# Two linear-attention blocks under one gate: the upper half of block A's q by seven products, woven with k chunks and a block of x^T phi(k)

## The chip, the cores and the metric

The kernel runs on one core of one Trainium2 chip. The metric is the device time of one execution in microseconds (us). Three runs of the kernel before took 188.43, 188.61 and 189.28, a median of 188.61.

## The reference

Two attention blocks, A and B, get the same x (2048 rows, 640 columns, bfloat16) with weights of their own. A gate mixes their outputs row by row:

```python
x = A_x
g = _sigmoid((x * gate_w).sum(-1, keepdims=True))
...
    phi = lambda t: jnp.where(t > 0, t + 1, jnp.exp(t)) + 1e-6
    pq, pk = phi(q), phi(k)
    kv = jnp.einsum("bhsd,bhse->bhde", pk, v)
    z = jnp.einsum("bhsd->bhd", pk)
    num = jnp.einsum("bhqd,bhde->bhqe", pq, kv)
    den = jnp.einsum("bhqd,bhd->bhq", pq, z)[..., None] + 1e-6
    o = num / den
...
return g * a + (1 - g) * b
```

q, k and v are x times a third of wqkv each, in 32 heads of 20 columns; a and b are o times wo of the block.

## The kernel before

**What is computed in which form.** v is never formed: kv is wv^T times G, where G = x^T phi(k) is 640 by 640. phi(k) lies in `pk` as 16 chunks of 128 rows, phi(q) transposed in `pqT[b]` as five blocks m of 128 features by 2048 rows. x lies in `xn` by rows and in `xT` transposed, in five blocks c of 128 columns. The gate's logits come from an extra column of A's k weights (column 320 of the second half) and are carried as `gl`, then `gf`.

**k.** `k_chunk` makes one of the 16 chunks: ten matmuls of 320 columns (L284) into a pair of PSUM banks (a slot), then phi. ScalarE (ACT) takes exp into `e` (L258), VectorE (DVE) clamps it (L263, "clamp"), and DVE takes the maximum of q + 1 and e (L272, "top"), reading PSUM. In the "lifted" form ACT also writes q + 1 to SBUF (L260), and DVE's top is a maximum of two bfloat16 tensors in SBUF (L267). The slot is then free once ACT has read it.

**q.** `q_unit` makes one block m for 1024 rows: ten matmuls of 512 columns (L336) and phi. `q_strassen` makes two blocks, m and m + 2, for the same 1024 rows by seven products in place of eight (Strassen's method, in the form with four sums on each side), for the contraction blocks c 0 to 3; block c = 4 is added in the ordinary way. That is 18 matmuls (L392) instead of 20. Its left sums are differences of weights, `TQ` (`tq_sums`, L376), its right ones sums of x^T, `SQ` (`sq_sum`, L369). It uses four single banks, `quad` = ce, cf, co, cz. A first product in ce is copied to co by ACT (L416); cz gets a second, which ACT copies to SBUF as p5 (L422); co accumulates further products, and DVE adds p5 to it twice (L410), into cf and into cz, where the accumulation goes on. Between the products, four pieces of other work ("fills") are called. Before, B's q is made so, with B's k chunks as fills, in the stage called weave; A's q is made in blocks and units.

**G.** The fifth 128-row block of G is an ordinary pass over the 16 chunks (`g_pass`, L468, tile gA: 32 matmuls of 320 columns). The other 512 rows are again seven products (`g_strassen`, L497, tiles gs): 16 matmuls of 320 columns each, from four sums of x, `SX` 1 to 4 (`x_sum`), and four of phi(k), `TK` 1 to 4 (`k_sum`); all of these, like other sums, go through `add_rows` (L647).

**The denominators.** `z_rows` sums phi(k) over the rows, from TK3 and TK4 (L567). `z_pass` brings it into place (L581, L582, L587). `rec_pass` multiplies it with phi(q) (L209, "den"), ACT takes Ln of both halves (L634), DVE adds the gate's logarithm `ge` (L638, tile d), ACT takes exp (L642). `norm_spread` spreads it over the partitions (L684, "ex", and ACT's copy to R, L689), and `scale` multiplies a block of `pqT` by R (L697).

**The gate.** `gate_rows` (L222 to L225) turns the 16 columns of logits into two logarithms, the last step being an Ln on ACT. `gate_spread` transposes them (L230, "gt"), ACT copies them (L232), and SyncE's DMA queue (SP) writes them out and reads them back as `ge` (L233, L236).

**Order.** The stretch of interest is scheduled by hand (`tc.manual_schedule()`): each engine executes its instructions in the order in which the program issues them, and waits where an operand is not ready. The order before, after the first chunks: lower rows of q blocks 0 to 3, lower rows of block 4, k chunks 8 to 15, the gate's rows, then

```python
        k_sum(0, 3)
        zr = q_pass([(m, 1) for m in range(DT)])
        wq[1] = load_w(1, "q", nc.sync)
        zsel = []
        g_pass(0, DT - 1, 3, lambda: zsel.append(z_pass(0, zr)), ST - CB)
        x_sum(2)
        x_sum(3)
        for k in range(1, 5):
            sq_sum(k, 1)
        g_strassen(0, lambda: zsel[0], 1, 3)
        tq_sums(1)
```

`q_pass` makes five units for the upper rows (`pqT[0]`, rows 1024 on), four of them lifted, with `k_sum` 2 and 4, `x_sum(1)`, `gate_spread` and `z_rows` between. PSUM has 8 banks; pools of slots are opened and closed stage by stage (`new_stage`), and a tile of a new pool waits for the last use of the tiles whose banks it takes. SP's order is: x^T by DMA transposes (L167, 15 of them), xn (L827), wv and wo of A, wk of B (when A's k is done), the gate's rows, wq of B (when A's q is done).

Of the kernel before, what the change touches and what calls it, by code (L numbers as in the profile page):

```python
# [9 lines left out]
P = 128  # L10
# [7 lines left out]
DT = D // P  # L18
# [16 lines left out]
def kernel(  # L35
# [33 lines left out]
    pools = {}  # L69
# [6 lines left out]
    def ps_raw(name, slot=None):  # L76

        if slot is None:
            slot = turn[0]
            turn[0] = (slot + 1) % 4  # L80
        return pools["ps"].tile([P, 4 * HB], BF16, tag=f"ps{slot}", name=name)

    def ps(name, slot=None):

        return ps_raw(name, slot).bitcast(FP32).rearrange("p (b n) -> p b n", b=2)
# [111 lines left out]

    warm_raw = ps_raw("warm", 3)
# [28 lines left out]
    def gate_spread():  # L227

        pt = ps("gt")
        nc.tensor.transpose(out=pt[0:2 * ST, 0, 0:P], in_=gf[:].rearrange("p b i -> p (b i)"), identity=ident32)  # L230
# [18 lines left out]
    class Phi:  # L249

        def __init__(self, dst, src, lifted=False):
            self.dst, self.src, self.lifted = dst, src, lifted
            e = work.tile([P] + list(dst.shape[1:]), BF16, tag="e", name="e", bufs=4)
            self.e = e[:]
            parts = [(self.e, dst, src)] if not isinstance(src, list) else [
                (self.e[:, n], dst[:, n], part) for n, part in enumerate(src)]
            for to, lifted_to, part in parts:
                nc.scalar.activation(out=to, in_=part, func=ACT.Exp)  # L258
                if lifted:
                    nc.scalar.activation(out=lifted_to, in_=part, func=ACT.Identity, bias=lift[:])  # L260
# [4 lines left out]
        def top(self):  # L265
            if self.lifted:
# [22 lines left out]
    def k_done(b, i, pt):  # L289
        f = Phi(pk[:, i, :].rearrange("p (b n) -> p b n", b=2), pt[:, :, 0:HF])  # L290
        if b == 0:
            nc.scalar.activation(out=gl[:, i:i + 1], in_=pt[:, 1, HF:HF + 1], func=ACT.Exp)
        f.clamp()
        f.top()

    def k_chunk(b, i, slot=None):
# [4 lines left out]
        k_done(b, i, pt)  # L301
# [69 lines left out]
    def tq_sums(b):  # L371
# [3 lines left out]
        for k, x, y in ((0, w12, w11), (1, w22, TQ[0]), (2, w22, w12), (3, w21, TQ[1])):  # L375
            nc.vector.tensor_tensor(out=TQ[k], in0=x, in1=y, op=ALU.subtract)  # L376

    def q_strassen(b, m, r, quad, fills):

        ce, cf, co, cz = quad  # L380
        lo, hi = 2 * r, 2 * r + 1
# [15 lines left out]
        def w_of(t):  # L397
            return lambda c: natural(c, t)
# [16 lines left out]
        prod(ce, w_of(m), x_of(lo), (0, 1), True)  # L415
        nc.scalar.copy(out=co, in_=ce)  # L416
# [11 lines left out]
        f.top()  # L428
# [3 lines left out]
        add(cz, co, p5[:])  # L432
        a.top()
# [39 lines left out]
    def x_sum(k):  # L473

        x11, x21 = [xn[:, 0:hc, n:n + ic] for n in (0, ic)]
        x12, x22 = [xn[:, hc:ST, n:n + ic] for n in (0, ic)]
        a, b, op = {
            1: (x21, x22, ALU.subtract), 2: (x11, SX[1], ALU.subtract),
            3: (x21, x11, ALU.subtract), 4: (x12, SX[2], ALU.subtract),
        }[k]  # L480
        add_rows(SX[k], a, b, op)
# [20 lines left out]
    def g_strassen(b, select, second, spare):  # L502
# [13 lines left out]
        even, odd = ps("gs0", 0), ps("gs1", second)  # L516
# [3 lines left out]
        if b == 1:  # L520
# [5 lines left out]
        else:  # L526
            rts = rec_pass(b, sel[0], 2)
        g_prod(odd, SX[2], TK[b][2], False, (lambda: sel.append(z_pass(1, zr))) if b == 1 else None)
# [7 lines left out]
        g_prod(even, x12, b21, False)  # L536
        nc.scalar.copy(out=lo[:, 0:2, :], in_=even[:, :, 0:HF])
        if b == 0:
# [5 lines left out]
        nc.scalar.copy(out=u3[:], in_=odd[:, :, 0:HF])  # L544
        if b == 1:
            add_rows(TM[0][:], M[0][:, :, HF:D], M[0][:, :, 0:HF], ALU.subtract)
        scale(b, 0)
        scale(b, 1)
        even = ps("gs0", 0)
        g_prod(even, SX[1], TK[b][1], True)  # L550
        add(hi[:, 2:4, :], even, u3)
        scale(b, 2)
        scale(b, 3)
        g_prod(odd, x22, TK[b][4], False)
        nc.scalar.copy(out=lo[:, 2:4, :], in_=odd[:, :, 0:HF])
        scale(b, 4)
# [241 lines left out]
    def q_pass(units):  # L798

        units = list(units)  # L800
        q_unit(0, *units.pop(0))
        for k in (2, 4):
            k_sum(0, k)
            q_unit(0, *units.pop(0), True)
            if k == 2:
                gate_spread()
        zs = []
        x_sum(1)
        q_unit(0, *units.pop(0), True)
        q_unit(0, *units.pop(0), True, behind=lambda: zs.append(z_rows(0)))  # L810
        zr = zs[0]
        sq_sum(4, 0)
        return zr

    with tc.manual_schedule():
        k_first()
        turn[0] = 2
        for n in range(2):
            for i in range(CB if n else 0, CB * 2 * n):
                k_chunk(0, i)  # L820
            for m in (0, 2):
                q_block(0, m, n, (lambda k: lambda: sq_sum(k, 0))(1 + m // 2) if n else None)
        q_unit(0, DT - 1, 0, True, None, lambda: sq_sum(3, 0))
        for i in range(hc, ST - 2):
            k_chunk(0, i)
    for n in range(1, NB):
        nc.sync.dma_start(  # L827
            out=xn[:, n * CB:(n + 1) * CB, :], in_=x2[n * HB:(n + 1) * HB, :].rearrange("(q p) d -> p q d", p=P)
        )
    wv[0] = load_w(0, "v", nc.sync)  # L830
    load_wo(0, nc.sync)

    def bank(pool, name, n=1):
        return pool.tile([P, HB] if n == 1 else [P, n, HB], FP32, tag=name, name=name)

    with tc.manual_schedule():
        k_chunk(0, ST - 2)
        turn[0] = (turn[0] + 1) % 4
        k_chunk(0, ST - 1)
        gate_rows()  # L840
# [12 lines left out]
        tq_sums(1)  # L853
        new_stage("weave")
        k_chunk(1, 0, 3)
        k_chunk(1, 1, 2)
# [12 lines left out]

        def chunk(i, slot):  # L870

            def go():
                pt = ps("kB", slot)
                for hf in range(2):
                    for c in range(DT):
                        k_mm(1, i, c, pt, hf)
                return Phi(pk[:, i, :].rearrange("p (b n) -> p b n", b=2), pt[:, :, 0:HF])

            return go
# [52 lines left out]
        k_chunk(1, 2, 3)  # L932
        fills = [chunk(3, 2), lambda: Masks(3)]
        fills += [chunk(i, 2 + i % 2) for i in range(4, ST)]
        fills.insert(13, lambda: fifth_two(1, 3))
        fills[14:] = [chunk(ST - 1, 2), lambda: None]
# [13 lines left out]
        g_strassen(1, None, 3, 1)  # L950
# [105 lines left out]
```

## Time and profile before

| | |
|---|---|
| median of three runs | 188.61 us |
| the profiled execution's own time | 187.96 us |
| its span, first to last instruction | 186.2 us |
| A's k chunks 8 to 15 on PE | 27.77 to 38.67 us |
| upper q of A, with gt | 38.67 to 49.57 |
| z, gA, first product of G's other rows | 49.57 to 57.23 |
| den to the end of A's G | 57.23 to 72.02 |
| B's k and q (weave) | 72.02 to 115.87 |
| after PE's last product | 180.41 to 186.2 |

The profile is one execution. Its busy times are sums over an engine's instructions. The chain of work follows the last instruction back to what released it, step by step, so that a step in it is time that the result waited for. PE is TensorE's matmuls, PEld its weight loads, which run beside them. Start times are us from the span's start. Instructions follow each other on an engine with a small overlap, so the distance between two starts can be less than the duration shown.

### The profile page before, as it was taken

What the parts mean: (1) busy time and instruction counts of PE and PEld (TensorE: products, weight loads), DVE (VectorE), ACT (ScalarE), POOL (GpSimd) and SP (SyncE); (2) the same over time, 40 slices, a digit from 0 to 9 for tenths busy, and PEclk for the clock granted to TensorE, in tenths of its full rate; (3) what the DMA queues carried; (4) which work ended last, traced back from release to release, by engine and by line L of the source; (5) the groups of instructions that cost most, each with busy time, mean ns of one, the idle gap of its engine ahead of it and who ended that gap; (6) DMA issues with size and microseconds to landing.
All of it is one profiled execution on the core that took longest, in us unless ns stands there. A gap on an engine that the chain in (4) does not pass through costs nothing.

```text
span 186.2 us, 3602 instructions
## 1 busy us (share of the span) xinstructions
PE 181.7 (98%) x1434; PEld 121.6 (65%) x1434; DVE 149.1 (80%) x265; ACT 90.2 (48%) x159; POOL 9.1 (5%) x25
## 2 busy tenths in 40 slices
PE   8999999999999999999999999999999999999993
PEld 3666657755577677576666655767678776777772
DVE  1378867889999499997989997969797989787554
ACT  2065488548924622546777776584712511111110
POOL 8920000000000000000000000000000000000000
PEclk9999999999999999999999999999999999999999
DMA  5975459992440000005000000144900003212122
GB/s 182 309 149 82 104 98 317 331 226 82 124 168 0 0 4 0 0 4 176 0 0 2 4 0 0 45 121 136 235 0 0 4 0 116 99 70 72 43 103 70
DMA packets 19769, 16.18 MB, mean 87 GB/s; under 512 B 8968, under 2 KB 19624, under 8 KB 19752
## 3 DMA queue, kind: packets, MB, share of 16 engines
q1 hardware_dynamic: 18888, 15.13, 29.3%
q10 hardware_dynamic: 864, 0.82, 1.3%
q8 instruction: 11, 0.18, 0.5%
q14 instruction: 6, 0.05, 0.1%
HBM read 10.52 MB, written 3.46 MB: 75 GB/s over the span
## 4 chain that ended last, share of the span: by engine, by line
PE 92%; DVE 3%; DMA 2%; ACT 1%; issue 0%; SPq 0%; DVEq 0%; ACTq 0%
PE gs L497 17%; PE kA L284 12%; PE qA L336 12%; PE kB L284 11%; PE q L392 7%; PE ox L708 6%; PE oy L708 5%; PE oz L708 5%; PE ow L708 3%; PE gB L468 2%; PE gA L468 2%; DMA wkA<-in_A_wqkv_dram 2%; PE qB L336 1%; PE q L336 1%; DVE osb L713 1%; PE kvA L894 1%
## 5 line engine op out<-in xcount | busy, mean ns | idle before, releaser
L284 PEld LDWEIGHTS <-xT 128*128 128x128 bf16 x320 | 31.0, 97 | 15.0 <-issue 0.5
L263 DVE TENSOR_SCALAR e<-e 128x640 bf16<-128x640 bf16 (+2 forms) x56 | 19.4, 346 | 7.3 <-ACT e L258 7.0
L284 PE MATMUL kB<-wkB,xT 128*128 128x320 bf16 x160 | 24.2, 299 | 0.0
L284 PE MATMUL kA<-wkA,xT 128*128 128x320 bf16 (+1 forms) x160 | 22.9, 299 | 0.4 <-ACT wkA L218 0.3
L336 PE MATMUL qA<-xT,wqA 128*128 128x512 bf16 x100 | 22.2, 379 | 0.0
L336 PEld LDWEIGHTS <-wqA 128*128 128x128 bf16 x100 | 11.7, 117 | 9.4
L258 ACT ACTIVATE e<-kA 128x640 bf16<-128x640 f32 x16 | 11.2, 707 | 9.7 <-PE kA L284 9.6
L497 PEld LDWEIGHTS <-xn 128*128 128x128 bf16 x128 | 12.3, 98 | 5.4 <-issue 0.9
L258 ACT ACTIVATE e<-kB 128x640 bf16<-128x640 f32 x16 | 11.3, 708 | 9.0 <-PE kB L284 8.9
L272 DVE SCALAR_TENSOR_TENSOR pk<-kA,e 128x640 bf16<-128x640 f32 x16 | 13.2, 824 | 2.6 <-DVE e L263 0.7
L272 DVE SCALAR_TENSOR_TENSOR pk<-kB,e 128x640 bf16<-128x640 f32 x16 | 13.2, 824 | 1.5
L752 ACT COPY u<-ox 128x320 f32<-128x320 f32 x8 | 3.4, 426 | 21.7 <-PE ox L708 21.7
L258 ACT ACTIVATE e<-q 128x512 bf16<-128x512 f32 x18 | 10.8, 598 | 5.4 <-PE q L392 3.8
L258 ACT ACTIVATE e<-qA 128x1024 bf16<-128x1024 f32 x10 | 10.2, 1023 | 5.1 <-PE qA L336 4.4
L708 PEld LDWEIGHTS <-xT 128*128 128x128 bf16 x85 | 8.0, 98 | 3.1 <-DVE xT L647 0.3
L708 PEld LDWEIGHTS <-pqTA 128*128 128x128 bf16 x85 | 7.9, 98 | 2.9 <-issue 0.2
L708 PEld LDWEIGHTS <-pqTB 128*128 128x128 bf16 x80 | 7.8, 98 | 3.0
L392 PE MATMUL q<-xT,wqB 128*128 128x512 bf16 x32 | 9.5, 379 | 0.0
L497 PE MATMUL gs<-pk,xn 128*128 128x320 bf16 x64 | 9.4, 299 | 0.0
L713 DVE TENSOR_TENSOR osb<-oz,u 128x320 bf16<-128x320 f32 (+1 forms) x18 | 8.0, 452 | 1.6 <-PE oz L708 0.9
L736 ACT COPY p1s<-ox 128x320 f32<-128x320 f32 x8 | 3.4, 426 | 10.2 <-PE ox L708 10.2
L697 DVE TENSOR_TENSOR pqTA<-pqTA,R 128x2048 bf16<-128x2048 bf16 x5 | 5.8, 1219 | 3.1 <-ACT R L689 3.1
(157 smaller groups left out, 316.1 us busy)
## 6 DMA issues: line engine op xcount, KB each, us to landing
out_dram<-osb SPq DMA_DIRECT2D x14, 160.0 KB, 1.9
xn<-in_A_x_dram SPq DMA_DIRECT2D x3, 640.0 KB, 5.5
wvA<-in_A_wqkv_dram SPq DMA_DIRECT2D x1, 800.0 KB
wkB<-in_B_wqkv_dram SPq DMA_DIRECT2D x1, 800.0 KB, 5.0
wqB<-in_B_wqkv_dram SPq DMA_DIRECT2D x1, 800.0 KB, 4.7
wvB<-in_B_wqkv_dram SPq DMA_DIRECT2D x1, 800.0 KB
MA<-m_rows SPq DMA_DIRECT2D x1, 800.0 KB, 4.6
woB<-in_B_wo_dram SPq DMA_DIRECT2D x1, 800.0 KB
```

What stands on the lines that cost most here:

```text
L258: nc.scalar.activation(out=to, in_=part, func=ACT.Exp)
L263: nc.vector.tensor_scalar(self.e, self.e, 1.0, EPS, op0=ALU.min, op1=ALU.add)
L272: nc.vector.scalar_tensor_tensor(out=dst, in0=src, scalar=1.0 + EPS, in1=e, op0=ALU.add, op1=ALU.max)
L284: nc.tensor.matmul(pt[:, hf, 0:n], lhsT=xT[:, c, i * P:(i + 1) * P], rhs=wk[b][:, c, hf * HF:hf * HF + n], start=(c == 0), stop=(c == DT - 1),
L336: nc.tensor.matmul(dst, lhsT=mixed(wq[b][:, c, :], m), rhs=xT[:, c, n * HB:(n + 1) * HB], start=first, stop=last,)
L392: nc.tensor.matmul(dst, lhsT=left(c), rhs=right(c), start=first and k == 0, stop=k == len(cs) - 1, skip_group_check=not first,)
L468: nc.tensor.matmul(pt[:, hf, 0:HF], lhsT=xn[:, i, c * P:(c + 1) * P], rhs=pk[:, i, hf * HF:(hf + 1) * HF], start=(i == 0), stop=(i == ST - 1),
L497: nc.tensor.matmul(pt[:, n, 0:HF], lhsT=left[:, i, n * P:(n + 1) * P], rhs=right[:, i, :], start=(first and i == 0), stop=(i == hc - 1), s ...
L697: nc.vector.tensor_tensor(out=pqT[b][:, m, :], in0=pqT[b][:, m, :], in1=rec, op=ALU.mult)
L708: nc.tensor.matmul(dst, lhsT=left[:, c, r0:r0 + P], rhs=right[:, c, :], start=(first and c == 0), stop=(c == DT - 1), skip_group_check=not ...
L713: nc.vector.tensor_tensor(out=dst, in0=acc, in1=sb, op=ALU.add)
L736: nc.scalar.copy(out=self.p1s[:], in_=self.at("x"))
```

## The change

The upper half of A's q is made by one lifted unit (block 4) and two calls of `q_strassen(0, m, 1, ...)`, for m = 0 and 1. The fills of the first are k chunks 13, 14, 15 and that unit; those of the second are the steps 0 to 9, 10 and 11, 12 and 13 of gA (and gt). The last steps of gA, 14 and 15, come after z. `q_strassen`'s first product and its copy become a function of their own, `q_lead`, so that the second group's can stand ahead of the unit's phi.

Around it:
- A's weight differences (`tq_sums(0)`) and the SQ sums of the upper rows stand between clamp and top of earlier chunks and blocks; the SQ sums of the lower rows, which only B needs, go into A's `g_strassen`. `x_sum` 1 and 2 are cut in two halves each.
- k chunks 8, 9, 11, 12, 14 and 15 of A and 0 to 3 of B are lifted. The unit's lift is "late": issued with its top, behind other ACT work.
- In A's `g_strassen`, z comes behind the first product, then the last gA steps, then the product of x12, and only then SX2's product and den. Before, the product of x12 stood between SX2's and SX3's.
- Half of B's weight differences come ahead of A's first `scale`; scales 3 and 4 of A come later, between B's first chunks.
- Slot 2 has a pool of its own, kept open across the stages "first", "joint" (the two groups) and "mid" (A's G).
- For A, the top of a group's first piece goes behind the second add.

```diff
     with tc.manual_schedule():
...
-                k_chunk(0, i)
+                k_chunk(0, i, None, False, (lambda k: lambda: tq_sums(0, [k]))(i // 2 - 2) if i in (5, 7) else None)
             for m in (0, 2):
-                q_block(0, m, n, (lambda k: lambda: sq_sum(k, 0))(1 + m // 2) if n else None)
-        q_unit(0, DT - 1, 0, True, None, lambda: sq_sum(3, 0))
...
+                q_block(0, m, n, (lambda k: lambda: tq_sums(0, [k]))(2 + m // 2) if n else None)
+        q_unit(0, DT - 1, 0, True, None, lambda: sq_sum(1, 1))
+        early = [(lambda k: lambda: sq_sum(k, 1))(k) for k in range(2, 5)] + [None, None]
+        for i in range(hc, ST - 3):
+            k_chunk(0, i, None, i in (8, 9, 11, 12), early[i - hc])
...
-        k_sum(0, 3)
-        zr = q_pass([(m, 1) for m in range(DT)])
+        q_strassen(0, 0, 1, quad, [
+            With(chunk(0, ST - 3, 2), ahead=lambda: x_sum(1, 0, 4)), With(chunk(0, ST - 2, 3, True), ahead=lambda: x_sum(1, 4, 8)), With(chunk(0, ST - 1, 2, True), gate_rows, lambda: k_sum(0, 3), lambda: x_sum(2, 0, 4)),
+            With(unit(DT - 1, 3), lambda: k_sum(0, 2))])
         wk[1] = load_w(1, "k", nc.sync)
...
+        q_strassen(0, 1, 1, quad, [With(g_part(0, 10)), With(g_part(10, 12), held["unit"].top, ahead=held["unit"].clamp), With(gated, lambda: k_sum(0, 4)),
+            With(lambda: None)], True)
         wq[1] = load_w(1, "q", nc.sync)
-        zsel = []
-        g_pass(0, DT - 1, 3, lambda: zsel.append(z_pass(0, zr)), ST - CB)
-        x_sum(2)
-        x_sum(3)
-        for k in range(1, 5):
-            sq_sum(k, 1)
-        g_strassen(0, lambda: zsel[0], 1, 3)
...
-        tq_sums(1)
+        x_sum(2, 4, 8)
+        g_strassen(0, 3, 0, 1, g_part(14, 16))
+
+        tq_sums(1, (2, 3))
...
-        k_chunk(1, 0, 3)
-        k_chunk(1, 1, 2)
+        k_chunk(1, 0, 3, True)
+        k_chunk(1, 1, 2, True)
+        scale(0, 3)
```

and in `g_strassen`, for A (b = 0):

```diff
-        g_prod(even, x11, b11, True, (lambda: sel.append(select())) if b == 0 else None)
+        g_prod(even, x11, b11, True)
         nc.scalar.copy(out=odd[:, :, 0:HF], in_=even[:, :, 0:HF])
...
+        if b == 0:
+            zr = z_rows(0, spare)
+            rest()
+            sq_sum(1, 0)
+            g_prod(even, x12, b21, False)
+            nc.scalar.copy(out=lo[:, 0:2, :], in_=even[:, :, 0:HF])
+            sq_sum(2, 0)
...
-            rts = rec_pass(b, sel[0], 2)
-        g_prod(odd, SX[2], TK[b][2], False, (lambda: sel.append(z_pass(1, zr))) if b == 1 else None)
+        g_prod(odd, SX[2], TK[b][2], False, lambda: sel.append(z_pass(b, zr)))
...
+            x_sum(3)
+            for k in (3, 4):
+                sq_sum(k, 0)
+            rts = rec_pass(b, sel[0], 2)
             k_sum(0, 1)
             x_sum(4)
-        norm_spread(b, rts, (2, spare))
+            tq_sums(1, (0, 1))
         g_prod(odd, SX[3], TK[b][3], False)
         u3 = temp("u3")
         nc.scalar.copy(out=u3[:], in_=odd[:, :, 0:HF])
+        if b == 0:
+            norm_spread(b, rts, (2, spare))
```

The new helpers only order calls: `With(go, *more, ahead=)` is a fill that calls `ahead` before the clamp and `more` after the top; `chunk` is a k chunk as a fill, `unit` a q unit as a fill with `q_lead` of the next group behind its matmuls, `g_part(lo, hi)` some steps of gA.

More of the change, by code (lines that the diff above doesn't have):

```diff
@@ L67, in new_stage @@
             pools["ps"] = held.enter_context(late_pool(name))
-    pools = {}
+    hold = ctx.enter_context(ExitStack())
+    pools = {2: hold.enter_context(late_pool("hold"))}
     new_stage("first")
@@ L196 @@
     make_identity(nc, ident32)
+    ps("unused", 2)
     warm_raw = ps_raw("warm", 3)
@@ L254, in __init__ @@
             self.e = e[:]
-            parts = [(self.e, dst, src)] if not isinstance(src, list) else [
+            self.parts = parts = [(self.e, dst, src)] if not isinstance(src, list) else [
                 (self.e[:, n], dst[:, n], part) for n, part in enumerate(src)]
@@ L258, in __init__, with lift @@
                 nc.scalar.activation(out=to, in_=part, func=ACT.Exp)
-                if lifted:
-                    nc.scalar.activation(out=lifted_to, in_=part, func=ACT.Identity, bias=lift[:])
+                if lifted is True:
+                    self.lift(lifted_to, part)
+        def lift(self, to, part):
+            nc.scalar.activation(out=to, in_=part, func=ACT.Identity, bias=lift[:])
         def clamp(self):
@@ L265, in top @@
         def top(self):
+            if self.lifted == "late":
+                self.lift(self.dst, self.src)
             if self.lifted:
@@ L287, in k_mm, with k_done @@
         )
-    def k_done(b, i, pt):
-        f = Phi(pk[:, i, :].rearrange("p (b n) -> p b n", b=2), pt[:, :, 0:HF])
+    def k_done(b, i, pt, lifted=False, between=None):
+        f = Phi(pk[:, i, :].rearrange("p (b n) -> p b n", b=2), pt[:, :, 0:HF], lifted)
         if b == 0:
@@ L293, in k_done, with k_chunk @@
         f.clamp()
+        if between is not None:
+            between()
         f.top()
-    def k_chunk(b, i, slot=None):
+    def k_chunk(b, i, slot=None, lifted=False, between=None):
         pt = ps(f"k{'AB'[b]}", slot)
@@ L300, in k_chunk @@
                 k_mm(b, i, c, pt, hf)
-        k_done(b, i, pt)
+        k_done(b, i, pt, lifted, between)
     def k_first():
@@ L369, in sq_sum, with tq_sums, q_lead, q_strassen @@
         nc.vector.tensor_tensor(out=SQ[:, k - 1, r], in0=a, in1=b, op=op)
-    def tq_sums(b):
+    def tq_sums(b, ks=range(4)):
         w = [[wq[b][:, c:c + 2, :].rearrange("p c (f t) -> p c t f", t=DT)[:, :, m:m + 2] for m in (0, 2)] for c in (0, 2)]
         (w11, w12), (w21, w22) = w
-        for k, x, y in ((0, w12, w11), (1, w22, TQ[0]), (2, w22, w12), (3, w21, TQ[1])):
+        for k in ks:
+            x, y = ((w12, w11), (w22, TQ[0]), (w22, w12), (w21, TQ[1]))[k]
             nc.vector.tensor_tensor(out=TQ[k], in0=x, in1=y, op=ALU.subtract)
-    def q_strassen(b, m, r, quad, fills):
+    def q_lead(b, m, r, quad):
+        for c in range(2):
+            q_mm(b, m, 2 * r, c, quad[0], c == 0, c == 1)
+        nc.scalar.copy(out=quad[2], in_=quad[0])
+    def q_strassen(b, m, r, quad, fills, led=False):
         ce, cf, co, cz = quad
+        if not led:
+            q_lead(b, m, r, quad)
         lo, hi = 2 * r, 2 * r + 1
@@ L427, in q_strassen @@
         f.clamp()
-        f.top()
+        if b == 1:
+            f.top()
         a = work_of()
@@ L432, in q_strassen @@
         add(cz, co, p5[:])
+        if b == 0:
+            f.top()
         a.top()
@@ L471, in g_mm, with x_sum @@
         )
-    def x_sum(k):
-        x11, x21 = [xn[:, 0:hc, n:n + ic] for n in (0, ic)]
-        x12, x22 = [xn[:, hc:ST, n:n + ic] for n in (0, ic)]
+    def x_sum(k, at=0, to=hc):
+        x11, x21 = [xn[:, at:to, n:n + ic] for n in (0, ic)]
+        x12, x22 = [xn[:, hc + at:hc + to, n:n + ic] for n in (0, ic)]
+        s1, s2 = [SX[n][:, at:to] for n in (1, 2)]
         a, b, op = {
-            1: (x21, x22, ALU.subtract), 2: (x11, SX[1], ALU.subtract),
-            3: (x21, x11, ALU.subtract), 4: (x12, SX[2], ALU.subtract),
+            1: (x21, x22, ALU.subtract), 2: (x11, s1, ALU.subtract),
+            3: (x21, x11, ALU.subtract), 4: (x12, s2, ALU.subtract),
         }[k]
-        add_rows(SX[k], a, b, op)
+        add_rows(SX[k][:, at:to], a, b, op)
     def k_sum(b, k):
@@ L500, in g_prod, with g_strassen @@
                 )
-    def g_strassen(b, select, second, spare):
+    def g_strassen(b, main, second, spare, rest=None):
         x11, x12 = [xn[:, k:k + hc, 0:ic] for k in (0, hc)]
@@ L535, in g_strassen @@
             k_sum(1, 1)
-        g_prod(even, x12, b21, False)
-        nc.scalar.copy(out=lo[:, 0:2, :], in_=even[:, :, 0:HF])
-        if b == 0:
+            g_prod(even, x12, b21, False)
+            nc.scalar.copy(out=lo[:, 0:2, :], in_=even[:, :, 0:HF])
+            norm_spread(b, rts, (2, spare))
+        else:
+            x_sum(3)
+            for k in (3, 4):
+                sq_sum(k, 0)
+            rts = rec_pass(b, sel[0], 2)
             k_sum(0, 1)
             x_sum(4)
-        norm_spread(b, rts, (2, spare))
+            tq_sums(1, (0, 1))
         g_prod(odd, SX[3], TK[b][3], False)
@@ L796, in load_wo, with clamp, __init__, __call__ @@
         eng.dma_start(out=wo_sb[b][:KG], in_=wo_dram[b].rearrange("(j p) f -> p j f", p=KG))
[L798 to L813, printed above, removed]
+    class Nothing:
+        def clamp(self):
+            pass
+        top = clamp
+    class With:
+        def __init__(self, go, *more, ahead=None):
+            self.go, self.more, self.ahead = go, more, ahead
+        def __call__(self):
+            return Both(self.go() or Nothing(), self.more, self.ahead)
+    class Both:
+        def __init__(self, f, more, ahead):
+            self.f, self.more, self.ahead = f, more, ahead
+        def clamp(self):
+            if self.ahead is not None:
+                self.ahead()
+            self.f.clamp()
+        def top(self):
+            self.f.top()
+            for go in self.more:
+                go()
+    def chunk(b, i, slot, lifted=False):
+        def go():
+            pt = ps(f"k{'AB'[b]}", slot)
+            for hf in range(2):
+                for c in range(DT):
+                    k_mm(b, i, c, pt, hf)
+            f = Phi(pk[:, i, :].rearrange("p (b n) -> p b n", b=2), pt[:, :, 0:HF], lifted)
+            if b == 0:
+                nc.scalar.activation(out=gl[:, i:i + 1], in_=pt[:, 1, HF:HF + 1], func=ACT.Exp)
+            return f
+        return go
+    def unit(m, slot):
+        def go():
+            pt = ps("qA", slot)
+            q_two(0, [(m, 2), (m, 3)], pt)
+            q_lead(0, 1, 1, quad)
+            held["unit"] = Phi(pqT[0][:, m, SH:S].rearrange("p (b n) -> p b n", b=2), pt, "late")
+        return go
+    def bank(pool, name, n=1):
+        return pool.tile([P, HB] if n == 1 else [P, n, HB], FP32, tag=name, name=name)
     with tc.manual_schedule():
@@ new lines @@
+        q_unit(0, DT - 1, 0, True, None, lambda: sq_sum(1, 1))
+        early = [(lambda k: lambda: sq_sum(k, 1))(k) for k in range(2, 5)] + [None, None]
+        for i in range(hc, ST - 3):
+            k_chunk(0, i, None, i in (8, 9, 11, 12), early[i - hc])
+        for n in range(1, NB):
+            nc.sync.dma_start(
+                out=xn[:, n * CB:(n + 1) * CB, :], in_=x2[n * HB:(n + 1) * HB, :].rearrange("(q p) d -> p q d", p=P)
+            )
+        wv[0] = load_w(0, "v", nc.sync)
+        load_wo(0, nc.sync)
@@ new lines @@
+        new_stage("joint")
+        ps("unused", 3)
+        quad = [cell(f"q{n}", n)[:] for n in range(4)]
+        held = {}
+        q_strassen(0, 0, 1, quad, [
+            With(chunk(0, ST - 3, 2), ahead=lambda: x_sum(1, 0, 4)), With(chunk(0, ST - 2, 3, True), ahead=lambda: x_sum(1, 4, 8)), With(chunk(0, ST - 1, 2, True), gate_rows, lambda: k_sum(0, 3), lambda: x_sum(2, 0, 4)),
+            With(unit(DT - 1, 3), lambda: k_sum(0, 2))])
+        wk[1] = load_w(1, "k", nc.sync)
+        held["g"] = ps("gA", 2)
@@ new lines, in g_part, with go, gated @@
+        def g_part(lo, hi):
+            def go():
+                for i in range(lo, hi):
+                    for hf in range(2):
+                        g_mm(DT - 1, i, hf, held["g"])
+                if hi == ST:
+                    for hf in range(2):
+                        nc.scalar.copy(out=GT[hf][:, DT - 1, :], in_=held["g"][:, hf, 0:HF])
+            return go
+        def gated():
+            g_part(12, 14)()
+            gate_spread(3)
+        q_strassen(0, 1, 1, quad, [With(g_part(0, 10)), With(g_part(10, 12), held["unit"].top, ahead=held["unit"].clamp), With(gated, lambda: k_sum(0, 4)),
+            With(lambda: None)], True)
@@ L854 @@
+        wq[1] = load_w(1, "q", nc.sync)
+        new_stage("mid")
+        pts = [ps(f"mid{n}", n) for n in (3, 0, 1)]
+        x_sum(2, 4, 8)
+        g_strassen(0, 3, 0, 1, g_part(14, 16))
+        tq_sums(1, (2, 3))
+        stage.pop().close()
+        hold.close()
+        del pools[2]
         new_stage("weave")
-        k_chunk(1, 0, 3)
-        k_chunk(1, 1, 2)
+        k_chunk(1, 0, 3, True)
+        k_chunk(1, 1, 2, True)
+        scale(0, 3)
         quad = [cell(f"q{n}", n)[:] for n in range(4)]
@@ L931 @@
         f.top()
-        k_chunk(1, 2, 3)
-        fills = [chunk(3, 2), lambda: Masks(3)]
-        fills += [chunk(i, 2 + i % 2) for i in range(4, ST)]
+        scale(0, 4)
+        k_chunk(1, 2, 3, True)
+        fills = [chunk(1, 3, 2, True), lambda: Masks(3)]
+        fills += [chunk(1, i, 2 + i % 2) for i in range(4, ST)]
         fills.insert(13, lambda: fifth_two(1, 3))
-        fills[14:] = [chunk(ST - 1, 2), lambda: None]
+        fills[14:] = [chunk(1, ST - 1, 2), lambda: None]
         for m, r in ((0, 0), (1, 0), (0, 1), (1, 1)):
```

53 lines of the change are left out of this document (17 added, 36 removed).

## The prediction

> **What bounds the kernel now.** I read the page's busy times and its chain first, then the chain in order of time, then busy time by stage, then the timeline where the edits fall.
>
> ```profile
> PE 181.7 (98%) x1434; PEld 121.6 (65%) x1434; DVE 149.1 (80%) x265; ACT 90.2 (48%) x159; POOL 9.1 (5%) x25
> ...
> PE 92%; DVE 3%; DMA 2%; ACT 1%; issue 0%; SPq 0%; DVEq 0%; ACTq 0%
> ```
>
> PE is busy nearly always and carries 92% of the chain that ended last. The chain in order of time (start, us, what) shows how full it is where the change falls:
>
> ```profile
> 38.67 4.32 PE qA L336 x20
> 42.99 0.11 PE gt L230
> 43.10 6.47 PE qA L336 x30
> 49.57 0.66 PE zA L567 x16
> ...
> 57.23 1.21 PE denA L209 x40
> 58.44 4.45 PE gs L497 x32
> 62.89 0.33 PE exA L684 x8
> 63.22 8.80 PE gs L497 x64
> 72.02 2.72 PE kB L284 x20
> 74.73 2.16 PE q L336 x10
> 76.89 1.51 PE kB L284 x10
> ```
>
> Twenty matmuls of 512 columns take 4.32 us, thirty take 6.47: 0.216 each without a gap. Ten of 320 take 1.36 (half of 2.72), sixteen of the g products 2.20 (8.80/4). No other engine stands in the chain between 28 and 72 us. So a matmul that goes is worth its 0.216, and a wait that comes is paid in full. The one gap nearby is in the last line: 1.51 instead of 1.36.
>
> The stages (columns: stage, its length, then busy us of PE, PEld, DVE, ACT, POOL; clock, DMA share, GB/s) show who is near to taking over:
>
> ```profile
> 30.00:40.00 10.00, 10.00 (x71) 6.88 (x70) 8.44 (x17) 5.86 (x16) 0.00 (x0) 1.00 1.04 306
> 40.00:50.00 10.00, 10.00 (x61) 5.35 (x59) 9.62 (x14) 7.75 (x10) 0.00 (x0) 1.00 0.45 140
> 50.00:60.00 10.00, 10.00 (x118) 7.17 (x111) 9.76 (x17) 4.33 (x9) 0.00 (x0) 1.00 0.28 85
> 60.00:70.00 10.00, 10.00 (x81) 6.93 (x79) 6.88 (x7) 4.36 (x7) 0.00 (x0) 1.00 0.01 2
> ```
>
> DVE has 0.6 us free between 40 and 60. PE does not wait for it there only because its results come early.
>
> **The change, part by part.**
>
> *Matmuls.* Before, the upper q of A is five units of ten 512-column matmuls: 50. After, one unit of 10 and two groups of 2+2+2+3+2+3+3+1 = 18: 46. Four fewer at 0.216: **-0.86 us**. Everything else PE does (16 k chunks, 32 matmuls of gA, seven g products, z, den, ex, gt) is the same in number and only reordered. The Trainium skill, TensorE: Matmul & The Clock Gate, section Back-to-back issue gap, gives about 131 ns a matmul at 512 columns in a stream of loads and matmuls; by it the four would be worth an estimated 0.52 and the sum below would be -0.38. The trace contradicts it, in the weave too: seven such matmuls of B's groups take 1.51 us in the chain, 0.216 each.
>
> *DVE's load from 17 to 71 us.* Two instructions that don't depend on each other start up to 0.09 us closer than one's duration (the four SQ sums of 0.68: 56.60, 57.32, 57.93, 58.53). In such steps: four weight differences for A (L376, 0.73) +2.6; four adds of a product to p5 (L410, 0.69) +2.4; phi of the upper q as four 512 pieces (0.32+0.60), two lifted pairs and one lifted unit (0.34+0.61) for four lifted units and one plain (0.43+1.15), +1.1; six k chunks whose top is a bf16 max after a lift by ACT. No row shows that max at 640 elements; the same form takes 0.69 at 1024 (L267) and 1.22 at 2048 (x_sum, L647). Bounds are 0.32 (the clamp of 640) and 0.69; a line through the two gives 0.49, which I take, 0.34 less than the 0.82 from PSUM, -2.0. Two scales go later (-2.3), two of B's weight differences come earlier (+1.3). Sum +3.1, against 7.7 us idle between 20 and 70 (50 minus 42.3 busy): it fits, if each result still comes in time. ACT gets +0.80 a lifted chunk (rows 0.69 at 512, 1.11 at 1024, the bounds): 0.60+0.70+0.05 = 1.35 from start to start, against PE's 1.36.
>
> *Each place where PE could wait,* in the changed order, with before's clock (handing over costs 0.04 to ACT or DVE, 0.06 to PE: DVE's top of the first B chunk ends at 76.83 and the chain resumes PE at 76.89):
> - The four weight differences and SQ sums of the upper rows lie between clamps and tops from 20 to 34 us. DVE waits for ACT there (24.55, 26.71, 28.86), so they cost nothing. The first SQ sum needs x^T of the last rows: that transpose is issued at 23.8 and lands in 3.5, 27.3; the sum is due at 29.2.
> - Group 1, first add: chunk 13's e waits for ACT's copy to 36.5, its top ends at 38.5, the add at 39.1; PE wants it after chunk 14, at 39.2. Margin 0.1.
> - The gate's Ln waits for chunk 15 through DVE and lies ahead of group 1's last pair in ACT's queue: Ln at 44.3, pair to 46.6, PE needs the bank at 47.9. Ten g steps hide 1.3 us.
> - Group 2, first add: p5 copy 0.58, add 0.69, handing over 0.14, in all 1.41 after the first product; PE has two and three matmuls and two g steps, 1.62. Margin 0.2. If that cover were gone, 1.4.
> - TK4 for z: from group 2's e on, DVE runs 5.5 us to its end, PE 5.7. Margin 0.2.
> - SP: gt moves from 43 to 51.6, and what stands behind it in SP's queue moves too. The gate's rows are back 6.2 after ACT's copy (45.2 to 51.4 before), at 58.2, due at 62.4. wqB, next in SP's queue, is issued near 55 and lands in 4.7, due at 65.6.
> - **TK1.** The product with x12 moves from behind den to ahead of it, so between den's end and the product with TK1 only SX3's product and ex are left: 2.20+0.33 = 2.53. Meanwhile these rows run (start, us, line):
>
> ```profile
> 58.49 0.84 ACT L634 ACTIVATE d<-denA,tiny 128x256 f32<-128x256 f32 x2 [0.49 <-PE denA L209]
> ...
> 59.13 0.75 DVE L638 SCALAR_TENSOR_TENSOR d<-d,ge 128x256 f32<-128x256 f32 x2
> 59.58 0.75 ACT L642 ACTIVATE rT<-d 128x256 bf16<-128x256 f32 x2 [0.25 <-DVE d L638]
> 59.80 1.48 DVE L647 TENSOR_TENSOR pqTB<-pk 128x2560 bf16<-128x2560 bf16 x1
> ```
>
> The last is TK1, queued behind both d on DVE. First Ln done 0.51 after den, second 0.88, second d at 0.92, TK1 from 1.27 to 2.75, PE at 2.82. PE waits **+0.29**; nothing is queued on PE that could go ahead. Before, 61.28 was 4 us early. From both sides: 0 if den's halves come out sooner, 0.6 if DVE is still at the SQ sums when d is due (by my count they end 0.3 after den, d is due at 0.55).
> - SX4: from den's end DVE needs 1.27+1.39+1.13+0.77+0.65+1.13+0.82+0.06 = 7.22 (TK1, x_sum 4, two weight differences, a scale, the add), PE 2.82+4.40 = 7.22. No more, but anything that DVE loses here shows.
> - B's chunks 0 to 3 lifted: ACT frees the bank, not DVE. The row at 76.89 waited for DVE's top at 76.01 (0.82); lifted, chunk 0's bank is free two us ahead. **-0.15**. The scales 3 and 4 put there (1.13 each) delay DVE; the copy that starts group 1 of B still ends 0.3 ahead of PE's need, and chunk 3's add 0.6 ahead.
>
> Sum: -0.86 + 0.29 - 0.15 = **-0.72 us**, with the rest of the kernel unchanged. The profiled execution took 187.96 (span 186.2, 1.8 around it): 187.24. The runs shown have a median of 188.61, 0.65 above that execution, with a spread of 0.85: **187.9** for a median.
>
> **The rivals.**
> - *No new wait, and B's start smoother* (the wait at TK1 is hidden, and the 0.11 that the five matmuls after kvA lose goes too: 1.19 instead of 1.08): -0.86-0.15-0.11 = -1.1, **187.5**. For it: margins hold elsewhere. Against: TK1's chain is made of rows.
> - *DVE becomes the bound between 30 and 46 us.* There I have it idle for only 0.5 us in 16. At the upper bounds, six maxes cost 0.20 more each (1.2), and lifts of 1.11 make ACT's step 1.65 against 1.36, 0.6 late by chunk 13. That is 1.8, less the 0.1 margin at group 1's first add: +1.7, so +1.0 and **189.6**, slower. It decides from 0.8 us of lag on. Against: in rows of one form at several sizes the time grows evenly with the size (L697 and L647 on DVE, 2048 and 2560 elements: 1.22 and 1.48). The Trainium skill, Perfetto Trace Analysis, section Identifying the Most-Contended Engine, says that matmul busy time shows badly how near a kernel is to its limit, while occupancy is a fair measure for VectorE. By that rule the 98% of PE prove little and DVE's 80% stand nearest to a limit; against it stand the chain's matmuls, 0.216 apart without a gap.
> - *The weave doesn't do what it says:* the three margins of 0.1 to 0.2 are missed by 0.2 each, since a group's product, copy and add follow each other. -0.72+0.6 = -0.1, **188.5**.
>
> **How the numbers follow.** Forecast 0.52, no new wait 0.23, DVE bound 0.13, weave missed 0.12. A half per cent, 0.94 us, is about what a measurement of this kernel can tell from no change. Faster: the second case and a little of the first's spread, 0.27. Within: 0.60. Slower: 0.13. The range runs from 187.3 (the smooth case and 0.2 of spread) to 189.2, into the DVE case.
>
> **What would show it.** 46 such matmuls at 0.216; an idle of some 0.3 us on PE ahead of the product with TK1, released by DVE; B's first chunk at 71.4 instead of 72.02, its third at 1.36; DVE busy about 45 us between 20 and 70. Wrong would be: PE waiting inside the two groups for an add, a copy or a lift; e of chunks 9 to 12 starting later and later after PE; the first SQ sum waiting for a DMA.

## The result, and the profile after

The changed kernel takes 187.6 us, the median of 20 runs (187.26 to 187.92). The kernel before, run beside it on the same chips, takes 188.31 (20 runs, 187.83 to 189.28). The ratio is 0.9963, with a 95% interval of 0.9954 to 0.9973: 0.7 us less. The profiled execution took 187.29 (span 185.6), against 187.96 (186.2).

The page of the changed kernel, busy time of each engine and the chain's shares:

```profile
PE 180.4 (97%) x1420; PEld 121.0 (65%) x1430; DVE 151.5 (82%) x279; ACT 98.0 (53%) x178; POOL 9.1 (5%) x25
...
PE 91%; DVE 4%; DMA 2%; ACT 1%; issue 1%; SPq 0%; DVEq 0%; ACTq 0%
```

PE has 1430 weight loads instead of 1434: four matmuls are gone. The 1420 for matmuls is not a count of work: ten records are missing, and each shows in the chain as a piece of 0.05 "issue". PE's busy time is 1.3 us less, but some 0.5 of that is the ten records. A second profile of the same kernel, whose chunk 8 starts 0.7 us later, has 181.7 again, so the gain can't be read from busy time. What is new is DVE's share of the chain, 4% instead of 3%. The chain in order of time shows where that lies (start, us, what):

```profile
39.23 1.15 PE q L410 x5
...
49.97 1.08 PE q L410 x5
...
60.77 1.24 PE denA L211 x40
62.03 0.85 ACT d L671 x2
62.90 0.43 DVE d L675
63.33 1.41 DVE pqTB L684
64.74 0.04 issue
64.78 6.75 PE gs L517 x48
71.53 2.72 PE kB L291 x20
...
76.41 1.36 PE kB L291 x10
```

Den ends at 62.01, and the chain then runs through both d and the sum TK1 (L684) before it is back on PE at 64.78. The five matmuls behind group 1's first add take 1.15, those of group 2 take 1.08 for the same work. B's third chunk takes 1.36. The timeline of the same stretch (start, us, engine, line; in brackets the idle time before and who ended it):

```profile
63.24 1.49 DVE L684 TENSOR_TENSOR pqTB<-pk 128x2560 bf16<-128x2560 bf16 x1
...
64.19 0.40 PE L721 MATMUL exA<-rT,spread 32*128 32x256 bf16 x8
...
64.78 2.33 PE L517 MATMUL gs<-pqTB,S 128*128 128x320 bf16 x16 [0.20 <-DVE pqTB L684]
66.95 2.34 PE L517 MATMUL gs<-pqTB,xn 128*128 128x320 bf16 x16
...
68.33 0.82 DVE L534 TENSOR_TENSOR GT<-gs,u 128x640 bf16<-128x640 f32 x1
...
69.20 2.33 PE L517 MATMUL gs<-pk,MB 128*128 128x320 bf16 x16
```

From ex to the product with TK1 it is 0.59 us from start to start, where ex alone needs 0.33: PE waits 0.26. The product with SX4 (69.20) starts just behind DVE's add, 2.25 after the product ahead of it (66.95); products that wait for nothing start 2.18 apart, as in the kernel before. That is another 0.07. And DVE's load by stage (columns as before):

```profile
50.00:60.00 10.00, 9.95 (x87) 6.73 (x87) 8.66 (x16) 6.28 (x12) 0.00 (x0) 1.00 0.48 132
60.00:70.00 10.00, 9.80 (x108) 6.70 (x107) 9.79 (x13) 5.51 (x9) 0.00 (x0) 1.00 0.02 7
```

The 9.95 for PE, also read in the two stages ahead, holds one missing record each; only the last, 9.80, has a real gap, the wait at TK1. DVE, slack there before at 6.88, is now at 9.79.

**Landmarks.** The time of an execution moves by 0.8 us with the first loads, as the last section shows. So I compare three intervals, all from the start of k chunk 8 (27.7 to 28.6 us into the span): W1 to B's first chunk, W2 to B's fifth (the chunk behind kvA), W3 to the last output matmul, near the span's end. Two profiles of the changed kernel agree in them within 0.02. Where a run's landmarks are given below, they are those of its one profile.

| kernel | W1 | W2 | W3 | median (runs) | ratio to before (95%) |
|---|---|---|---|---|---|
| before | 44.25 | 57.00 | 151.95 | 188.31 (20) | |
| changed | 43.78 | 56.38 | 151.33 | 187.6 (20) | 0.9963 (0.9954 to 0.9973) |
| changed, again | 43.80 | 56.39 | 151.35 | 187.73 (12) | 0.9973 (0.9960 to 0.9986) |
| four_more | 44.59 | 57.19 | 152.14 | 188.53 (12) | 1.0010 (0.9998 to 1.0023) |
| tk1_early | 43.47 | 56.18 | 151.14 | 187.56 (8) | 0.9959 (0.9943 to 0.9975) |
| b_plain | 43.80 | 56.91 | 151.86 | 188.17 (12) | 0.9995 (0.9981 to 1.0009) |
| dve_late | 44.34 | 56.93 | 151.89 | 188.34 (12) | 1.0001 (0.9988 to 1.0013) |
| x12_late | 43.89 | 56.49 | 151.44 | 187.82 (12) | 0.9981 (0.9968 to 0.9993) |
| before_tq | 44.25 | 56.84 | 151.79 | 188.24 (12) | 0.9998 (0.9985 to 1.0011) |
| before_lift | 44.24 | 56.83 | 151.79 | 188.25 (12) | 0.9992 (0.9978 to 1.0007) |
| tk1_tail | 43.46 | 56.05 | 151.01 | 187.25 (6) | 0.9941 (0.9929 to 0.9953) |
| three_waits | 43.39 | 55.99 | 150.94 | 187.20 (6) | 0.9943 (0.9928 to 0.9957) |

Before to changed: W1 falls by 0.47 and W2 by 0.62, so another 0.15 goes between B's first and fifth chunk. W3 falls by 0.62 too: nothing behind that gives any of it back. Within W1 the changed kernel has three waits of 0.07 (group 1's first add), 0.26 (TK1) and 0.07 (SX4). With four matmuls at 0.216 that makes -0.86 + 0.40 = -0.46.

### The profile page after: what moved, and what is told of

The parts are those of the page before. It is cut to its first block, busy times and chain, and to the rows that moved or that the text cites. A ratio compares the mean times of both kernels' runs of the same rounds, so it can differ in the third digit from the quotient of the medians.

```text
span 185.6 us, 3617 instructions
## 1 busy us (share of the span) xinstructions
PE 180.4 (97%) x1420; PEld 121.0 (65%) x1430; DVE 151.5 (82%) x279; ACT 98.0 (53%) x178; POOL 9.1 (5%) x25
## 4 chain that ended last, share of the span: by engine, by line
PE 91%; DVE 4%; DMA 2%; ACT 1%; issue 1%; SPq 0%; DVEq 0%; ACTq 0%
PE gs L517 16%; PE kA L291 12%; PE kB L291 11%; PE q L410 10%; PE qA L345 7%; PE ox L745 6%; PE oy L745 5%; PE oz L745 5%; PE ow L745 3%; PE gB L487 2%; PE q L345 2%; PE gA L487 2%; DMA wkA<-in_A_wqkv_dram 2%; PE qB L345 1%; DVE osb L750 1%; PE kvA L979 1%
## 5 line engine op out<-in xcount | busy, mean ns | idle before, releaser
L260 ACT ACTIVATE e<-q 128x512 bf16<-128x512 f32 x26 | 15.6, 598 | 5.4 <-PE q L410 4.3
L517 PEld LDWEIGHTS <-xn 128*128 128x128 bf16 x128 | 12.3, 98 | 5.6 <-issue 0.6
L345 PE MATMUL qA<-xT,wqA 128*128 128x512 bf16 x57 | 13.3, 379 | 0.2
L345 PEld LDWEIGHTS <-wqA 128*128 128x128 bf16 x64 | 7.5, 117 | 5.9
L279 DVE SCALAR_TENSOR_TENSOR pk<-kB,e 128x640 bf16<-128x640 f32 x12 | 9.9, 822 | 1.0
L279 DVE SCALAR_TENSOR_TENSOR pk<-kA,e 128x640 bf16<-128x640 f32 x10 | 8.2, 822 | 0.9
L428 DVE TENSOR_TENSOR q<-q,p 128x512 f32<-128x512 f32 x12 | 8.3, 692 | 0.2 <-ACT p L438 0.2
L487 PEld LDWEIGHTS <-xn 128*128 128x128 bf16 x64 | 6.2, 98 | 3.4 <-issue 0.7
L260 ACT ACTIVATE e<-qA 128x1024 bf16<-128x1024 f32 x6 | 6.2, 1027 | 4.2 <-PE qA L345 3.9
```

The costliest lines, as they stand in the source:

```text
L345: nc.tensor.matmul(dst, lhsT=mixed(wq[b][:, c, :], m), rhs=xT[:, c, n * HB:(n + 1) * HB], start=first, stop=last,)
L428: nc.vector.tensor_tensor(out=dst, in0=src, in1=sb, op=ALU.add)
L487: nc.tensor.matmul(pt[:, hf, 0:HF], lhsT=xn[:, i, c * P:(c + 1) * P], rhs=pk[:, i, hf * HF:(hf + 1) * HF], start=(i == 0), stop=(i == ST - 1),
L517: nc.tensor.matmul(pt[:, n, 0:HF], lhsT=left[:, i, n * P:(n + 1) * P], rhs=right[:, i, :], start=(first and i == 0), stop=(i == hc - 1), s ...
```

## The experiments

My theory was this sum of matmuls and waits. The rivals were a cheaper matmul (0.13), DVE as the real bound, and a gain at B's third chunk that comes from something other than the lift.

**The changed kernel again**, unedited, for the scatter.

> The changed kernel as it is, as the measure for its variants on the same chip. Both theories: its runs as before, 0.4% under the kernel before; a wait of about 0.26 us of TensorE ahead of the product with TK1, first chunk of B at 71.5 us.

Chunk 8 started at 28.44 instead of 27.75, yet W1, W2 and W3 came out 0.02, 0.01 and 0.02 longer. Two later variants of the kernel before, whose edits take no work from PE in W1, repeat its 44.25 within 0.01 as well. A difference of 0.05 in the landmarks can be read; one of 0.05 in the total can't.

**Four matmuls put back.**

```diff
-        for c in range(2):
+        for c in (0, 1, 0, 1) if b == 0 else (0, 1):
             q_mm(b, m, 2 * r, c, quad[0], c == 0, c == 1)
```

> Each of A's two groups runs its leading product twice (the second run of the two matmuls overwrites the first), so four 512-column matmuls more and the result unchanged. Theory (time is TensorE's count at 0.216 us plus its waits): 0.86 us slower than the changed kernel, level with the kernel before but for the wait gained and lost, and B's first chunk at 72.4. Rival (matmuls in a weave cost less than in a run, or the stretch is bound by VectorE's sums and tops): 0 to 0.5 us slower.

W1 rose by 0.81, and all of it stayed to the end (W3 +0.81). The wait at group 1's first add is hidden by the two matmuls ahead of it (its five take 1.09 here), so four cost 0.81 + 0.06 = 0.87, or 0.22 each. The Trainium skill (TensorE: Matmul & The Clock Gate, section Back-to-back issue gap) gives about 131 ns for one, which would have made an estimated +0.52; the run decides against it.

**TK1 and three SQ sums earlier, one SQ sum later**, so that DVE is free for d and TK1.

```diff
-            sq_sum(1, 0)
+            k_sum(0, 1)
             g_prod(even, x12, b21, False)
...
-            sq_sum(2, 0)
...
-            for k in (3, 4):
+            for k in (1, 2):
                 sq_sum(k, 0)
             rts = rec_pass(b, sel[0], 2)
-            k_sum(0, 1)
             x_sum(4)
             tq_sums(1, (0, 1))
+            sq_sum(3, 0)
...
         if b == 1:
             scale(b, 3)
+        else:
+            sq_sum(4, 0)
```

> TK1 is made ahead of den, where the two first SQ sums of the lower rows stood; these four SQ sums come later. Theory (VectorE's TK1 behind both d costs TensorE 0.26 us, and SX4's product another 0.07 behind the add): the wait ahead of the product with TK1 is gone, B's first chunk at 71.2, 0.3 us faster than the changed kernel. Rival (another result is as late, the spread of the reciprocals or SX4): the wait shows up ahead of ex, SX1 or SX4 instead and the time stays within 0.1 us.

The waits at TK1 and SX4 are both gone: W1 is 0.31 shorter. But W2 is only 0.20 shorter. The chain shows the 0.12 that came back:

```profile
72.03 2.84 PE kB L291 x20
```

B's first two chunks take 2.84 instead of 2.72. In the timeline the last two adds of G stand behind the fourth SQ sum on DVE:

```profile
71.81 0.69 DVE L378 TENSOR_TENSOR SQ<-xT,SQ 128x1024 bf16<-128x1024 bf16 x1
72.41 0.88 DVE L597 TENSOR_TENSOR GT<-gs,u 128x320 bf16<-128x320 f32 x2
```

They start 0.38 after B's first chunk, where the changed kernel starts them 0.04 after it. They end at 73.29, and PE's weight loads for B's second chunk, which had stopped, go on at 73.35: the adds seem to free its bank. The next run tests that.

**The same, with that sum behind B's last weight differences.**

```diff
-        else:
-            sq_sum(4, 0)
...
         tq_sums(1, (2, 3))
+        sq_sum(4, 0)
```

> TK1 ahead of den as in tk1_early, with the fourth SQ sum behind B's last weight differences instead of between A's scales. Theory (in tk1_early that sum held up the last two adds of A's G and so the bank of B's second chunk, 0.12 us): from the entry of the long stretch to B's first chunk as in tk1_early, and the two first chunks of B in 2.72 instead of 2.84, so 0.12 us faster than tk1_early and 0.32 faster than the changed kernel. Rival (the 0.12 us come from elsewhere in B): 2.84 stays.

The two chunks take 2.72 again, W1 stays 0.32 shorter and W2 is 0.33 shorter. So the place of that one sum of 0.68 us made the difference.

**Also the add of group 1 ahead of a top.** Group 1's first add goes ahead of the top of the fill before it, for A.

```diff
         a.clamp()
-        a.top()
+        if b == 1:
+            a.top()
         prod(cz, tq(1), sq(1), (0, 1), True)
...
         add(cf, co, p5[:])
+        if b == 0:
+            a.top()
```

> As tk1_tail, and in A's groups the first add goes ahead of the top of the first fill, so that it follows p5 at once. Theory (the first add of group 1 is 0.07 us late in the changed kernel: five matmuls take 1.15 instead of 1.08): the 1.15 becomes 1.08, no wait of TensorE for VectorE is left between A's k chunks and B's third chunk, 0.4 us faster than the changed kernel and 0.55% under the kernel before. Rival (VectorE, late by the delayed top, misses a later handover): 1.08 there, but a wait at chunk 14's or 15's matmuls or at TK4.

Its chain from den on:

```profile
62.07 2.28 PE gs L520 x16
64.35 0.33 PE exA L723 x8
64.68 6.63 PE gs L520 x48
```

PE goes straight from den into the products, and nothing of ACT or DVE stands between. The five matmuls of group 1 take 1.08. W1 is 43.39, 0.86 under before: what four matmuls at 0.216 give. With every wait gone the whole price of the matmuls is seen. By the landmarks this is the best version run: 0.39 under the changed kernel in W3. Its median of 187.20 is 0.57% under before (0.43% to 0.72%); from tk1_tail's 187.25, six runs each, it can't be told. The add's new place is worth 0.07 (W1 43.46 to 43.39), the rest 0.32.

**B's chunks 0 to 3 not lifted.**

```diff
-        k_chunk(1, 0, 3, True)
-        k_chunk(1, 1, 2, True)
+        k_chunk(1, 0, 3)
+        k_chunk(1, 1, 2)
```

and likewise chunks 2 and 3.

> B's k chunks 0 to 3 are not lifted: VectorE takes their tops from PSUM, as in the kernel before. Theory of the prediction (lifting them takes away the wait of 0.15 us ahead of B's third chunk): the wait is back, 0.15 us slower, and more if the copy that opens B's first group is late behind the longer tops. Rival (two weight differences moved ahead of A's scales took it away): VectorE ends the top of B's first chunk near 74.9, 1.5 us before its bank is wanted; no wait, time within 0.05 us unless the later copy waits.

My reason for the lift fell here. The third chunk takes 1.36 from 76.42 without the lift too. The loss comes later, in the timeline at kvA:

```profile
80.72 0.82 DVE L279 SCALAR_TENSOR_TENSOR pk<-kB,e 128x640 bf16<-128x640 f32 x1
...
81.60 2.03 PE L979 MATMUL kvA<-GT,wvA 128*120 128x120 bf16 x35 [0.36 <-DVE pk L279]
```

kvA takes the bank of B's third chunk, and DVE frees it only at 81.54: the chain ahead of it is DVE's, with the scales 3 and 4 at 1.13 each among its steps. W2 is 0.53 longer than in the changed kernel, which leaves 0.09 of the change's 0.62.

**One part alone in the kernel before: two of B's weight differences earlier.**

```diff
             x_sum(4)
+            tq_sums(1, (0, 1))
...
-        tq_sums(1)
+        tq_sums(1, (2, 3))
```

> The kernel before, with only two of B's four weight differences moved ahead of A's first scale, into the 3.1 us in which VectorE waits for R. Rival to the prediction's step on B's chunks: the wait of 0.15 us ahead of B's third chunk goes, 0.15 us faster than the kernel before. Prediction's step (it takes the lift): VectorE's top still holds the bank, though 1.4 us earlier; by its own rows that is early enough, so a wait left over would mean that ScalarE or the bank's order sets it.

**The other part alone: B's chunks 0 to 3 lifted in the kernel before.**

```diff
-        k_chunk(1, 0, 3)
-        k_chunk(1, 1, 2)
+        k_chunk(1, 0, 3, True)
+        k_chunk(1, 1, 2, True)
```

and likewise chunks 2 and 3.

> The kernel before, with only B's k chunks 0 to 3 lifted. Prediction's step: ScalarE frees the bank, the wait of 0.15 us ahead of B's third chunk goes, 0.15 us faster than the kernel before. Rival: the lift writes the same rows of phi(k) that A's last sums read, so ScalarE waits for VectorE and some of the wait stays.

Each alone makes the third chunk 1.36 and W2 0.16 and 0.17 shorter, with W1 as before. Either is enough for that 0.15, and the two together in the changed kernel give it once. What the lift is needed for there is kvA's bank, with the scales 3 and 4 now ahead of it.

**DVE later at group 1**: the sum of x placed there is made twice.

```diff
-ahead=lambda: x_sum(1, 0, 4))
+ahead=lambda: (x_sum(1, 0, 4), x_sum(1, 0, 4)))
```

> The first half of x_sum 1 is computed twice ahead of chunk 13's clamp, 0.6 us more on VectorE, result unchanged. Theory (the first add of group 1 is 0.1 us ahead of TensorE, and VectorE's only slack there is the 0.17 us wait for chunk 13's e): the add ends 0.43 later, TensorE waits about 0.35 us ahead of group 1's third product from co, 0.35 us slower than the changed kernel. Rival (the weave has slack for VectorE to be late): no wait, within 0.1 us.

W1 rose by 0.56, not by 0.35. PE's first matmul behind the add, in the timeline:

```profile
40.36 0.59 PE L410 MATMUL q<-SQ,MB 128*128 128x512 bf16 x2 [0.46 <-DVE q L428]
```

PE waits for exactly that add. The repeated sum writes the same tile again and starts 0.72 after the first, where 0.6 was expected. DVE's clamp behind it came 0.77 after the sum's start in the changed kernel and comes 1.33 after it here: 0.16 of DVE's own idle time took up a part, and the other 0.56 reached PE in full. The add was 0.07 late there already; the margin of 0.1 that was expected did not exist.

**The product with x12 behind den again**, where it covers d and TK1.

```diff
-            g_prod(even, x12, b21, False)
-            nc.scalar.copy(out=lo[:, 0:2, :], in_=even[:, :, 0:HF])
...
             rts = rec_pass(b, sel[0], 2)
+            g_prod(even, x12, b21, False)
+            nc.scalar.copy(out=lo[:, 0:2, :], in_=even[:, :, 0:HF])
             k_sum(0, 1)
```

> The product of x12 goes back between SX2's product with den and SX3's, as it stood in the kernel before. Theory: 2.2 us of cover are back between den and the product with TK1, whose wait of 0.26 us and SX4's 0.07 are gone; but z's place has lost that cover, and z_pass waits for zE by about 0.2 us. Net 0.1 us faster than the changed kernel. Rival (z needs the cover more than TK1): z_pass waits 0.4 us or more, and the kernel is slower than the changed one.

I expected 0.1 less; W1 rose by 0.11. The waits between 55 and 62 us show why (engine and line, who it waited for, us in total, times, longest):

```profile
PEld L618 <- DVE zE L608: 0.6, 1, 0.6
```

The product was also the cover for z. Without it PE reaches z's matmuls while DVE is still at zE (until 57.57), and PE waits:

```profile
57.62 0.21 PE L618 MATMUL zA<-I,zE 128*128 128x32 bf16 x1 [0.23 <-DVE zE L608]
```

It starts 1.48 after the start of the eight matmuls ahead of it (56.14) instead of 1.09: 0.39 lost. den loses nothing more: it starts 1.18 after the matmuls ahead of it in both kernels. So the move saves the 0.33 at TK1 and SX4, and loses that and 0.1 more at z.

## Why the prediction was right, step by step

- **Four matmuls, -0.86.** Right, and shown twice: 0.86 in W1 with every wait gone, 0.87 for four put back.
- **TK1, +0.29.** Right in cause and size: 0.26. The time from 62.54 (first d) to 64.73 (TK1's end) is the chain of rows that the prediction strung together.
- **SX4, "no more".** Off by 0.07. Both sides of that step came to 7.22, with no margin; DVE's add ended at 69.15, when PE could have gone at 69.13, and handing over came on top. A tie was booked as no wait; the step named its risk, that anything DVE loses there shows.
- **Group 1's first add, margin 0.1.** DVE's top ended at 38.48 and the add at 39.09, forecast at 38.5 and 39.1. But PE's need, forecast at 39.2, was the end of chunk 14 (39.24), and a matmul starts before the one ahead of it has ended: by 0.15 us at this place in three_waits, where PE waits for nothing. So PE came at 39.07 and could go at 39.14: the margin was -0.07. Five matmuls at 1.15 instead of 1.08 are the price. PE waiting inside a group for an add was one of the prediction's signs of being wrong; of the three margins that the third rival doubted, only this one was missed, by 0.07 and not 0.2.
- **B's third chunk, -0.15.** The size is right, the reason is one of two: the step said "lifted, chunk 0's bank is free two us ahead", and b_plain has the same 1.36 without the lift, because two weight differences had left DVE's queue ahead of that top. The prediction counted that move in DVE's load, but not at this place. The lift pays at kvA, which the prediction did not name: 0.53 without it. So the prediction credited the lift with a gain that either move gives (before_tq, before_lift).
- **The sum, -0.72.** -0.62 by the landmarks: the two small waits of 0.07 and a TK1 0.03 cheaper than thought. In the medians it is 0.7, with an interval of 0.5 to 0.9; that this comes closer to 0.72 than the landmarks do is luck. The prediction took 0.94 us for about what a measurement can tell from no change; here 0.7 is told from it. The forecast of 187.9 stood on a median of 188.61 from three runs, whose 20 put it at 188.31; that is the 0.3 between 187.9 and 187.6.
- **What was costed at nothing** held: the Ln at 44.31 and the last pair to 46.67 (44.3 and 46.6 forecast), group 2 without a wait (1.08), no wait for TK4, wqB issued at 55.31 (near 55), the first SQ sum at 29.19 without a wait for a DMA. The maximum of two bfloat16 tensors of 640 elements took 0.49 as estimated, the lift 0.79 (0.80). DVE is busy 45.7 us between 20 and 70 (45).
- **DVE as the bound** did not happen, but the rival was near: dve_late shows that lag at group 1 is paid in full from the start, where the rival left it a margin of 0.1. (Its 0.8 less that margin is the 0.7 that the change was to gain.) The rule named there (the Trainium skill, Perfetto Trace Analysis, section Identifying the Most-Contended Engine), that matmul busy time is a poor sign, was read as pointing away from PE; here PE's 98% was what it looked like, since each matmul taken away or added moved the end by its full 0.22, once the waits are counted.
- **No new wait** was half right as a rival: its -0.86 and -0.15 are there to be had, but by the two reorderings of three_waits (W3 -1.01), not by themselves. Its third term, the 0.11, was not gained: the five matmuls behind kvA take 1.19 in every chain read, three_waits too. The timeline of three_waits has a hint. kvA's 35 weight loads run without a pause from 80.46 to 82.61, and the load for the next product starts at 82.64 together with its matmul, where at group 1 of A it starts 0.14 ahead (39.09 and 39.23). That would make the 0.11 PE's own; no run was made on it, and the cause stays open.

## What to carry to other kernels

Where one engine fills the chain without a gap, price removed work at its start-to-start time, and then look for the waits that its removal uncovers. Here two of the three were at places where need and supply came out within 0.1 of each other, and a tie there is a wait by the handing over. Before crediting a gain to an edit, list every other edit that would give it: two parts each gave the same 0.15 alone, and one of them was really paying elsewhere.

When a step that covers a wait is to be moved, list everything that it covers; the product with x12 was worth more ahead of z than ahead of TK1. A sum that nothing needs soon should stand in its engine's queue behind what frees a bank, even if it is only 0.68 us.

## What the runs showed of the hardware

The start differs between executions far more than the rest. Chunk 8 began between 27.72 and 28.56 us in the twelve profiles, with the first loads ahead of it, while the intervals behind it repeat within 0.02 in two profiles of one kernel. A change of 0.07 can so be read from a trace where the totals of runs spread by 0.8.

On DVE the sum made twice into one tile started 0.72 after its first copy, while two independent ones of the same 0.68 start 0.60 apart (61.08 and 61.68 in the changed kernel). A repeated instruction put in as a known load so costs more than one in a stream.
